# Attention with a maxout FFN on one core: K and Q through one transpose bank, two steps of software pipelining, weights in column halves

## The chip, the core and the metric

The kernel runs on one core of a Trainium2 chip. The metric is the device time of one execution in microseconds (us). Engines are named as in the profile's rows: PE is TensorE (PEld its weight loads), DVE is VectorE, ACT is ScalarE, POOL is GpSimd, SP is SyncE, which issues most transfers. [...]

## What is computed

```python
# q, k, v: (4, 8, 768, 64); n_sink = 4, window = 64; heads 0, 2 and 6 are "retrieval" heads
scores = q @ k.T / sqrt(64)
causal = rel >= 0                                    # rel = query position - key position
stream = causal & (key < n_sink | rel < window)
a = softmax(where(retrieval head, causal, stream), scores)
x = (a @ v).transpose(0, 2, 1, 3).reshape(3072, 512)
h = maximum(maximum(x @ w1, x @ w2), x @ w3)         # w1, w2, w3: 512 x 768
out = h @ w_out                                      # w_out: 768 x 512, out 3072 x 512
```

## The kernel before

The work is cut into 32 **steps**. Step s is a batch entry, a half of its 768 tokens (384, three blocks of 128) and a pair of heads; four steps (four pairs of heads) make a half, two halves a batch entry. A **first-half step** has 384 queries on 384 keys (two score units), a **second-half step** 384 queries on 768 keys (four score units). When a half's four steps are done, its 384 x 512 rows of x go through the FFN, which is cut into 24 **units** by a generator (`ffn`, L206): 18 times four matmuls of 384 columns, for three weight matrices and six blocks of 128 hidden columns, and three output tiles of six matmuls of 512 columns that count two units each. FFN units are laid between the pieces of later steps by `share` (L410), which spreads 168 units evenly over steps 7 to 32; the last half's 24 come behind everything.

The schedule is manual: every engine executes its instructions in the order in which the program writes them, so the loop at L424 sets the order on every queue. One pass s of that loop:

- `load(s + 7)` (L108): K, Q and V of a step, four transfers on SyncE's queue, into a pool of 8.
- `prep(s + 1)` (L269): VectorE casts K and Q to fp16 (`kn`, `qn`).
- `scores(s, [0, 1])` (L313): score matmuls on TensorE into PSUM tiles `st` (a pool of two), exponentials on ScalarE into `pt`, masks by GpSimd's multiplications with `mk`.
- `av(s - 1)` (L360): probabilities times V on TensorE into `oacc`; VectorE's reciprocal `rc` and product `x`.
- `scores(s, [2, 3])` in second-half steps.
- `turn_x(s - 1)` (L387): three transposes of x on TensorE into `tr`, a copy to `xT` by VectorE.
- `turn(s + 1, 1)` and `turn(s + 1, 0)` (L292): for K, then for Q, three transposes into `tr` and a copy to `KT` or `QT` by VectorE, whose result has a stride of three elements.
- `prep_v(s + 1)` (L278): V to fp16 by VectorE (`va`), and GpSimd's product `vf` of V with the far mask `fm`, for key blocks that are far from the query.

Between the pieces stand five calls of `share`. The pool `trp` holds one PSUM bank, so each of the three turns of a step waits until the copy of the one ahead has emptied it. The FFN's PSUM pool `fsp` holds two tiles; ScalarE takes away the first matrix's product (`acc`, L231) and the output tiles (`ot`, L248), VectorE takes the two maxima (L234). In steps 0 to 3 `head_consts` (L177) adds, per pair of heads, four mask operations of 256 columns and the copy `fm` on VectorE. The weights are four transfers that GpSimd issues, three behind step 0 and one behind step 2.

Of the kernel before, what the change touches and what calls it, by code (L numbers as in the profile page):

```python
# [48 lines left out]
def kernel(  # L49
# [14 lines left out]
    nc = tc.nc  # L64
# [24 lines left out]
    xp = ctx.enter_context(tc.tile_pool(name="xp", bufs=2))  # L89
# [37 lines left out]
    load(0)  # L127
    ir32 = consts.tile([P, 2 * H], mybir.dt.int32, name="ir32")
    nc.sync.dma_start(
# [3 lines left out]
    for s in range(1, AHEAD):  # L133
        load(s)


    ident = consts.tile([P, P], FP16, name="ident")
    make_identity(nc, ident)
# [8 lines left out]
    win = consts.tile([P, 256], FP16, name="win")  # L147
    nc.gpsimd.affine_select(
        out=win, in_=base, compare_op=ALU.is_gt, fill=0.0,
        base=window, pattern=[[-1, 256]], channel_multiplier=1,  # L150
    )
    win0 = consts.tile([P, 256], FP16, name="win0")
    nc.vector.tensor_copy(out=win0, in_=win)
    if n_sink > 0:
        nc.vector.tensor_copy(out=win0[0:n_sink, :], in_=base[0:n_sink, :])
    full = consts.tile([P, 256], FP16, name="full")
    nc.vector.tensor_tensor(out=full, in0=base, in1=win, op=ALU.subtract)
    full0 = consts.tile([P, 256], FP16, name="full0")
    nc.vector.tensor_tensor(out=full0, in0=base, in1=win0, op=ALU.subtract)
# [6 lines left out]
    RT = consts.tile([P, H], FP32, name="RT")  # L166
    nc.vector.tensor_copy(out=RT, in_=ir32[:, 0 : 2 * H : 2])

    far = consts.tile([P, H, 4], FP32, name="far")
    nc.vector.tensor_copy(out=far, in_=RT.unsqueeze(2).to_broadcast([P, H, 4]))  # L170
    if n_sink > 0:
        nc.vector.memset(far[0:n_sink, :, 0:1], 1.0)

    mk = consts.tile([P, H, 512], FP16, name="mk")
    fm = consts.tile([P, H, 4, D + 1], FP16, name="fm")

    def head_consts(hp):  # L177
# [87 lines left out]
    KTs = {}  # L265
    QTs = {}
    cast = {}

    def prep(s):  # L269
        b, half, hp = where(s)  # L270
        ks_, qs, vs = staged.pop(s)
# [4 lines left out]
        cast[s] = (qn, kn, vs)  # L276

    def prep_v(s):  # L278
        b, half, hp = where(s)
        vs = cast[s][2]  # L280
        j, k0 = b % 2, half * HB
        hs = slice(2 * hp, 2 * hp + 2)
        if s < NHP:
            head_consts(hp)
        nc.vector.tensor_copy(out=va[j][:, hs, k0 : k0 + HB, 0:D], in_=vs)  # L285
# [6 lines left out]
    def turn(s, which):  # L292
        b, half, hp = where(s)
        src = cast[s][which]
        tr = trp.tile([P, 1024], FP16, tag="tr", name="tr")
        for j in range(HB):
            nc.tensor.transpose(  # L297
                tr[:, j * P : (j + 1) * P], src[:, j].rearrange("p h d -> p (h d)"), ident
            )
        if which == 0:  # L300
            t = QTs[s] = qkt.tile([P, HALF], FP16, tag="QT", name="QT")
        else:
            if half == 0:
                KTs[b, hp] = qkt.tile([P, S], FP16, tag=f"KT{hp}", name=f"KT{hp}")
            t = KTs[b, hp][:, half * HALF : (half + 1) * HALF]
        nc.vector.tensor_copy(  # L306
            out=t.rearrange("p (t j) -> p j t", j=HB),
            in_=tr[:, 0:HALF].rearrange("p (j t) -> p j t", j=HB),
        )
# [3 lines left out]
    def scores(s, us):  # L313
        b, half, hp = where(s)
        QT, KT = QTs[s], KTs[b, hp]
# [4 lines left out]
        for u in us:  # L320
            st = sps.tile([P, 2, 512], FP32, tag="st", name="st")
            sts.append(st)
            for ki, q0, n, c0 in UNITS[half][u]:
                for hl in range(2):
                    hb = D * hl
                    nc.tensor.matmul(  # L326
                        st[:, hl, c0 : c0 + n * P],
                        KT[hb : hb + D, ki * P : (ki + 1) * P],
                        QT[hb : hb + D, q0 * P : (q0 + n) * P],
                        start=True, stop=True,  # L330
                    )
# [72 lines left out]

    FIRST = 7
    units = (2 * B - 1) * 24
    done = 0.0
    emitted = 0

    def share(s, part, parts):  # L410
        nonlocal emitted
        if s < FIRST or s >= NSTEP + 1:
            return
        want = units * ((s - FIRST) + (part + 1) / parts) / (NSTEP + 1 - FIRST)
        n = int(want) - emitted
        if n > 0 and queue:
            fill(n)
            emitted += n

    prep(0)  # L420
    turn(0, 1)
    turn(0, 0)
    prep_v(0)
    for s in range(NSTEP + 1):  # L424
# [66 lines left out]
```

## Time and profile before

| | |
|---|---|
| median of 3 runs | 281.4 us (280.76 to 281.68) |
| profiled execution: time | 280.9 us |
| profiled execution: span (first to last instruction) | 280.8 us |
| busy: PE, PEld, DVE, ACT, POOL | 214.8, 125.8, 179.3, 117.9, 126.5 us |
| chain that ended last, by engine | PE 58%, DVE 27%, issue 5%, ACT 4% |
| first scores of steps 0, 5, 8, 31 start at | 9.78, 45.66, 70.81, 249.14 us |
| HBM read, written | 25.17 MB, 6.29 MB |

The profile is one execution. A row of the timeline gives start, duration, engine, line, operation, output and inputs, and in brackets how long the engine was idle before and what ended that. Matmuls are pipelined and their ends modelled, so a matmul's cost in a row of them is read from start to start.

### The profile page before, as it was taken

The numbers are of one execution on the slowest core, as the hardware profiler recorded it, in microseconds if no ns is written. First come the engines' busy times: TensorE is split into PE (matmuls) and PEld (weight loads), VectorE is DVE, ScalarE is ACT, GpSimd is POOL, SyncE is SP. The second block draws the span as 40 slices with busy tenths as digits, with TensorE's granted clock in tenths as the row PEclk, the third lists the DMA queues.
The fourth block names the chain that finished last, engine by engine and source line by source line (L and its number), as shares of the span: only waits on it lengthen the run. The fifth ranks groups of instructions, "written<-read, shape, count | busy, mean of one in ns | idle before, by whom it ended". The sixth has DMA issues, their size and how long they took to land.

```text
span 280.8 us, 5222 instructions
## 1 busy us (share of the span) xinstructions
PE 214.8 (76%) x2000; PEld 125.8 (45%) x2000; DVE 179.3 (64%) x381; ACT 117.9 (42%) x169; POOL 126.5 (45%) x141
## 2 busy tenths in 40 slices
PE   0333366668888889889898888897788878989994
PEld 0222234435554545454445444554455435555551
DVE  2878855455786776667767774667668853664360
ACT  1222234553334364565244357653342347553322
POOL 2366455444555543455455454446354445253000
PEclk9999999999999999999999999999999999999999
DMA  6999999321103920293017511720020011000202
GB/s 159 268 280 213 220 247 259 96 66 51 30 0 105 275 73 4 87 251 98 16 58 220 151 25 75 215 78 2 37 76 2 0 40 75 4 0 2 112 0 112
DMA packets 49000, 28.65 MB, mean 102 GB/s; under 512 B 27216, under 2 KB 45904, under 8 KB 48976
## 3 DMA queue, kind: packets, MB, share of 16 engines
q1 hardware_dynamic: 46608, 25.18, 32.1%
q0 software_dynamic: 2368, 3.15, 6.3%
q8 instruction: 15, 0.25, 0.4%
q14 instruction: 9, 0.07, 0.1%
HBM read 25.17 MB, written 6.29 MB: 112 GB/s over the span
## 4 chain that ended last, share of the span: by engine, by line
PE 58%; DVE 27%; issue 5%; ACT 4%; DMA 2%; SPq 2%; POOL 0%; DVEq 0%; ACTq 0%
PE yy L223 21%; PE yy L241 10%; PE st L326 8%; PE oacc L371 7%; PE tr L297 7%; DVE QT L306 5%; DVE KT L306 5%; DVE xT L399 3%; DVE acc L234 3%; ACT pt L334 3%; DVE mk L180 3%; DVE hT L234 3%; PE yst L223 2%; PE tr L396 2%; DVE x L381 1%
## 5 line engine op out<-in xcount | busy, mean ns | idle before, releaser
L356 POOL TENSOR_TENSOR pt<-pt,mk 128x512 f16<-128x512 f16 (+1 forms) x96 | 100.7, 1071 | 56.9 <-ACT pt L334 56.7
L334 ACT ACTIVATE pt<-st 128x1024 f16<-128x1024 f32 x96 | 82.8, 917 | 75.6 <-PE st L326 71.0
L287 POOL TENSOR_TENSOR vf<-va,fm 128x390 f16<-128x390 f16 (+1 forms) x32 | 20.9, 654 | 71.7 <-DVE va L285 71.7
L231 ACT CAST acc<-yy 128x384 f16<-128x384 f32 x45 | 21.7, 482 | 51.2 <-PE yy L223 46.8
L326 PE MATMUL st<-QT,KT 64*128 64x384 f16 (+2 forms) x320 | 31.2, 309 | 13.7 <-DVE QT L306 13.3
L234 DVE TENSOR_TENSOR acc<-yy,acc 128x384 f16<-128x384 f32 x45 | 25.0, 556 | 22.2 <-PE yy L223 14.8
L223 PE MATMUL yy<-xT,w0t 128*128 128x384 f16 x180 | 37.4, 331 | 0.1
L223 PE MATMUL yy<-xT,w2t 128*128 128x384 f16 x180 | 36.6, 326 | 0.8 <-ACT acc L231 0.6
L223 PE MATMUL yy<-xT,w1t 128*128 128x384 f16 x180 | 37.2, 330 | 0.0
L306 DVE COPY KT<-tr 128x384 f16<-128x384 f16 x32 | 25.6, 801 | 13.7 <-PE tr L297 13.5
L297 PE MATMUL tr<-ident,kn 128*128 128x128 f16 x96 | 11.7, 238 | 27.9 <-DVE xT L399 19.1
L306 DVE COPY QT<-tr 128x384 f16<-128x384 f16 x32 | 25.5, 798 | 10.5 <-PE tr L297 10.5
L241 PE MATMUL yy<-woutt,hT 128*128 128x512 f16 x132 | 31.8, 379 | 0.0
L371 PEld LDWEIGHTS <-pt 128*128 128x128 f16 x672 | 27.6, 104 | 6.2 <-issue 2.3
L371 PE MATMUL oacc<-va,pt 128*128 128x65 f16 x352 | 28.3, 204 | 0.0
L326 PEld LDWEIGHTS <-KT 64*128 64x128 f16 x320 | 13.8, 100 | 32.0 <-issue 18.1
L234 DVE TENSOR_TENSOR hT<-yy,acc 128x384 f16<-128x384 f32 x45 | 24.9, 554 | 4.4 <-PE yy L223 2.8
L248 ACT COPY ot<-yy 128x512 f32<-128x512 f32 x22 | 12.9, 588 | 26.2 <-PE yy L241 23.4
L371 PE MATMUL oacc<-vf,pt 128*128 128x65 f16 x320 | 23.7, 203 | 0.0
L297 PEld LDWEIGHTS <-kn 128*128 128x128 f16 x96 | 8.6, 105 | 32.1 <-issue 23.0
L223 PEld LDWEIGHTS <-w2t 128*128 128x128 f16 x192 | 17.2, 97 | 11.7 <-issue 2.9
L223 PEld LDWEIGHTS <-w0t 128*128 128x128 f16 x192 | 16.9, 98 | 11.8 <-issue 3.4
(44 smaller groups left out, 185.1 us busy)
## 6 DMA issues: line engine op xcount, KB each, us to landing
ks<-in_k_dram SPq DMA_DIRECT2D x32, 192.0 KB, 3.8
qs<-in_q_dram SPq DMA_DIRECT2D x32, 192.0 KB, 4.0
vs<-in_v_dram SPq DMA_DIRECT2D x64, 96.0 KB, 3.8
out_dram<-ot SPq DMA_DIRECT2D x24, 256.0 KB, 2.0
w0t<-in_moe_w_dram POOLq DMA_DIRECT2D x1, 768.0 KB, 9.9
w1t<-in_moe_w_dram POOLq DMA_DIRECT2D x1, 768.0 KB, 13.9
w2t<-in_moe_w_dram POOLq DMA_DIRECT2D x1, 768.0 KB, 17.8
woutt<-in_moe_w_out_dram POOLq DMA_DIRECT2D x1, 768.0 KB, 10.7
```

What stands on the lines that cost most here:

```text
L223: nc.tensor.matmul(yy[:, 0:HALF], w_t[wi][:, ks, ni * P : (ni + 1) * P], xT[b, half][ks], start=(ks == 0), stop=(ks == KS - 1),)
L231: nc.scalar.copy(out=acc, in_=yy[:, 0:HALF])
L234: nc.vector.tensor_tensor(out=dst, in0=yy[:, 0:HALF], in1=acc, op=ALU.max)
L241: nc.tensor.matmul(yo[:, 0:DMdl], hT[ns][:, tb * P : (tb + 1) * P], woutt[:, ns, :], start=(ns == 0), stop=(ns == NNB - 1),)
L248: nc.scalar.copy(out=ot, in_=yo[:, 0:DMdl])
L287: nc.gpsimd.tensor_tensor(out=vf[j][:, hs, k0:k1, 0 : D + 1], in0=va[j][:, hs, k0:k1, 0 : D + 1], in1=fm[:, hs, k0:k1], op=ALU.mult,)
L297: nc.tensor.transpose(tr[:, j * P : (j + 1) * P], src[:, j].rearrange("p h d -> p (h d)"), ident)
L306: nc.vector.tensor_copy(out=t.rearrange("p (t j) -> p j t", j=HB), in_=tr[:, 0:HALF].rearrange("p (j t) -> p j t", j=HB),)
L326: nc.tensor.matmul(st[:, hl, c0 : c0 + n * P], KT[hb : hb + D, ki * P : (ki + 1) * P], QT[hb : hb + D, q0 * P : (q0 + n) * P], start=True, ...
L334: nc.scalar.activation(out=pt[:, u, :, 0:w], in_=st[:, :, 0:w], func=AF.Exp, scale=sc)
L356: nc.gpsimd.tensor_tensor(out=x, in0=x, in1=m, op=ALU.mult)
L371: nc.tensor.matmul(o[:, qi, hl, 0 : D + 1], pt[:, u, hl, c : c + P], vv[:, 2 * hp + hl, ki, 0 : D + 1], start=(idx == 0), stop=(idx == len ...
```

## The change

K and Q of a step are transposed into one bank one after the other and leave it by one copy of 768 columns, into one tile `KQ` (`turn(s)`). Casts run two steps ahead instead of one, and Q's cast is ScalarE's. The transposes of x belong to step s - 2 and stand right behind the first scores; K and Q of step s + 1 are turned before AV instead of at the end of the step. FFN units are spread from step 5 instead of 7, with weights of 5 for a first-half and 7 for a second-half step. Masks are one operation of 512 columns per head; `fm` goes, its place in the product `vf` is taken by `far`, broadcast. V's cast in the first four steps is ScalarE's. The weight matrices come in column halves, seven transfers behind step 1. The flags' transfer moves to ScalarE's queue.

```diff
-    xp = ctx.enter_context(tc.tile_pool(name="xp", bufs=2))
+    xp = ctx.enter_context(tc.tile_pool(name="xp", bufs=3))
...
-    load(0)
     ir32 = consts.tile([P, 2 * H], mybir.dt.int32, name="ir32")
-    nc.sync.dma_start(
+    nc.scalar.dma_start(
...
+    warm = consts.tile([P, 2], FP32, name="warm")
+    nc.vector.memset(warm, 0.0)
+    nc.scalar.activation(out=warm, in_=warm, func=AF.Exp)
...
+    def head_masks(hp):
+        for h in (2 * hp, 2 * hp + 1):
+            nc.vector.scalar_tensor_tensor(
+                out=mk[:, h], in0=F, scalar=RT[:, h : h + 1], in1=W,
+                op0=ALU.mult, op1=ALU.add,
+            )
...
-    def head_consts(hp):
...
+    def load_weights():
+        for c in (0, DF // 2):
+            for wt, w in zip(w_t, (moe_w1, moe_w2, moe_w3)):
+                nc.gpsimd.dma_start(
+                    out=wt[:, :, c : c + DF // 2],
+                    in_=w[:, c : c + DF // 2].rearrange("(ks p) n -> p ks n", p=P),
+                )
+        nc.gpsimd.dma_start(
+            out=woutt, in_=moe_w_out.rearrange("(ns p) m -> p ns m", p=P)
+        )
...
         nc.vector.tensor_copy(out=kn, in_=ks_.rearrange("p h j d -> p j h d"))
-        nc.vector.tensor_copy(out=qn, in_=qs.rearrange("p h j d -> p j h d"))
+        nc.scalar.copy(out=qn, in_=qs.rearrange("p h j d -> p j h d"))
...
+        if s < NHP:
+            nc.scalar.copy(out=vdst, in_=vs)
+        else:
+            nc.vector.tensor_copy(out=vdst, in_=vs)
...
-            in1=fm[:, hs, k0:k1], op=ALU.mult,
...
+            in1=far[:, hs, k0:k1].unsqueeze(3).to_broadcast([P, 2, k1 - k0, D + 1]),
+            op=ALU.mult,
...
+    def turn(s):
         tr = trp.tile([P, 1024], FP16, tag="tr", name="tr")
+        for i, x in enumerate(cast.pop(s)):
+            for j in range(HB):
+                c = i * HALF + j * P
+                nc.tensor.transpose(
+                    tr[:, c : c + P], x[:, j].rearrange("p h d -> p (h d)"), ident
+                )
+        half = where(s)[1]
+        KQs[s] = qkt.tile(
+            [P, S], FP16, tag=f"KQ{half}", name="KQ", bufs=2 if half else NHP + 3
+        )
         nc.vector.tensor_copy(
+            out=KQs[s].rearrange("p (i t j) -> p i t j", i=2, j=HB),
+            in_=tr[:, 0:S].rearrange("p (i j t) -> p i t j", i=2, j=HB),
         )
...
+    FIRST = NHP + 1
+    weight = [0 if s < FIRST else (5, 7)[where(s)[1]] for s in range(NSTEP)] + [3]
...
-        if s + 1 < NSTEP:
-            prep(s + 1)
         if live:
             n_u = len(UNITS[where(s)[1]])
             scores(s, [0, 1])
-        share(s, 0, 5)
-        if s > 0:
+        if s > 1:
+            turn_x(s - 2)
+        share(s, 1, 7)
+        if s + 1 < NSTEP:
+            turn(s + 1)
+        share(s, 3, 7)
+        if 0 < s <= NSTEP:
             av(s - 1)
-        share(s, 1, 5)
+        if s + 2 < NSTEP:
+            prep(s + 2)
         if live and n_u > 2:
             scores(s, [2, 3])
...
         if s + 1 < NSTEP:
+            prep_v(s + 1)
+        if s + 2 < NHP:
+            head_masks(s + 2)
+        share(s, 6, 7)
+        if s == 1:
+            load_weights()
```

VectorE's queue over one first-half step in the middle of the program, before. The rows run from the copy of x (`xT`) of one step to that of the next; the maxima of FFN units are the rows of L234:

```order
L399 COPY xT_1958<-tr 128x384
L306 COPY KT_1971<-tr 128x3x128
L306 COPY QT<-tr 128x3x128
L285 CAST va_164<-vs 128x2x3x64
L274 CAST kn<-ks 128x384
L275 CAST qn<-qs 128x384
L379 RECIPROCAL rc<-oacc 128x6
L381 TENSOR_TENSOR x<-oacc,rc 128x384
L234 TENSOR_TENSOR acc<-yy,acc 128x384
L399 COPY xT_1959<-tr 128x384
```

The same queue over a first-half step now (maxima are the rows of L230):

```order
L399 COPY xT_1998<-tr 128x384
L230 TENSOR_TENSOR acc<-yy,acc 128x384
L303 COPY KQ<-tr 128x768
L230 TENSOR_TENSOR hT_1909<-yy,acc 128x384
L379 RECIPROCAL rc<-oacc 128x6
L381 TENSOR_TENSOR x<-oacc,rc 128x384
L268 CAST kn<-ks 128x384
L281 CAST va_171<-vs 128x2x3x64
L230 TENSOR_TENSOR acc<-yy,acc 128x384
L230 TENSOR_TENSOR hT_1910<-yy,acc 128x384
L399 COPY xT_1999<-tr 128x384
```

The two copies of K and Q behind the copy of x became one, a maximum stands between, and `qn` is gone from this queue.

GpSimd's queue around the weights, before, from `vf` of step 1 to the first mask of step 1:

```order
L287 TENSOR_TENSOR vf0_166<-va0_164,fm_176 128x2x3x65
L194 DMA w0t_177<-in_moe_w1_dram 128x4x768
L194 DMA w1t_178<-in_moe_w2_dram 128x4x768
L194 DMA w2t_179<-in_moe_w3_dram 128x4x768
L356 TENSOR_TENSOR pt_262<-pt_262,mk_175 128x2x256
```

The same queue now, from `vf` of step 2 to its last transfer:

```order
L283 TENSOR_TENSOR vf0_173<-va0_171,far_167 128x2x3x65
L191 DMA w0t_177<-in_moe_w1_dram 128x4x384
L191 DMA w1t_178<-in_moe_w2_dram 128x4x384
L191 DMA w2t_179<-in_moe_w3_dram 128x4x384
...
L195 DMA woutt_180<-in_moe_w_out_dram 128x6x512
L356 TENSOR_TENSOR pt_311<-pt_311,mk_170 128x2x256
```

The three transfers moved behind `vf` of step 2 and became six of half the width (the second three read like the first), `woutt` follows at once, and the masks of step 2 stand behind all seven.

## Rows read from the trace of the kernel before

**Rows 1.** The page, part 1: busy time, share of the span, instructions.

```profile
PE 214.8 (76%) x2000; PEld 125.8 (45%) x2000; DVE 179.3 (64%) x381; ACT 117.9 (42%) x169; POOL 126.5 (45%) x141
```

**Rows 2.** Windows: busy us of PE, PEld, DVE, ACT, POOL; clock, DMA share, GB/s.

```profile
0.00:45.66 45.66, 16.27 (x135) 9.39 (x136) 30.89 (x71) 10.89 (x13) 23.76 (x33) 1.00 1.04 234
...
70.81:249.14 178.33, 151.50 (x1467) 88.79 (x1467) 123.40 (x260) 84.23 (x124) 87.61 (x93) 1.00 0.27 79
```

**Rows 3.** Waits of PE from 61 to 261 us: total us, times, longest us.

```profile
PE tr L297 <- DVE xT L399: 16.4, 24, 1.3
PE st L326 <- DVE QT L306: 6.2, 16, 0.9
PE tr L297 <- DVE KT L306: 4.6, 14, 0.9
```

**Rows 4.** Timeline of PE, a first-half step (19): start, us, what.

```profile
153.01 0.50 PE L326 MATMUL st<-QT,KT 64*128 64x384 f16 x6 [0.24 <-DVE QT L306]
153.45 0.82 PE L223 MATMUL yy<-xT,w2t 128*128 128x384 f16 x4
154.11 0.35 PE L371 MATMUL oacc<-va,pt 128*128 128x65 f16 x6
...
154.48 0.81 PE L223 MATMUL yy<-xT,w0t 128*128 128x384 f16 x4
...
157.58 0.33 PE L297 MATMUL tr<-ident,kn 128*128 128x128 f16 x3 [0.75 <-DVE xT L399]
157.75 0.81 PE L223 MATMUL yy<-xT,w0t 128*128 128x384 f16 x4
```

**Rows 5.** Timeline of PE, a second-half step (13).

```profile
107.65 0.61 PE L326 MATMUL st<-QT,KT 64*128 64x384 f16 x8 [0.24 <-DVE QT L306]
108.19 0.82 PE L223 MATMUL yy<-xT,w2t 128*128 128x384 f16 x4
...
109.50 0.23 PE L371 MATMUL oacc<-vf,pt 128*128 128x65 f16 x2
...
110.45 0.81 PE L223 MATMUL yy<-xT,w1t 128*128 128x384 f16 x4
```

**Rows 6.** Timeline of DVE in the middle of the program.

```profile
157.18 0.35 DVE L399 COPY xT<-tr 128x384 f16<-128x384 f16 x1
...
159.16 0.80 DVE L306 COPY QT<-tr 128x384 f16<-128x384 f16 x1 [0.42 <-PE tr L297]
159.82 0.34 DVE L285 CAST va<-vs 128x384 f16<-128x384 f32 x1
...
160.72 0.56 DVE L234 TENSOR_TENSOR hT<-yy,acc 128x384 f16<-128x384 f32 x1
161.19 0.54 DVE L274 CAST kn<-ks 128x384 f16<-128x384 f32 x1
...
162.13 0.20 DVE L379 RECIPROCAL rc<-oacc 128x6 f32<-128x6 f32 x1
```

**Rows 7.** Groups of ACT by line and form: count, busy us, mean ns, idle before.

```profile
L334 ACT ACTIVATE pt<-st 128x1024 f16<-128x1024 f32 x64 | 63.8, 1024 | 75.6 <-PE st L326 71.0 <-POOL vf L287 4.6
```

**Rows 8.** Timeline of POOL at the start.

```profile
17.81 0.90 POOL L287 TENSOR_TENSOR vf<-va,fm 128x390 f16<-128x390 f16 x1 [2.16 <-DVE va L285]
18.65 0.94 POOL L194 DMA_DIRECT2D w0t<-in_moe_w_dram  x1
...
20.32 0.75 POOL L194 DMA_DIRECT2D w2t<-in_moe_w_dram  x1
21.08 2.89 POOL L356 TENSOR_TENSOR pt<-pt,mk 128x512 f16<-128x512 f16 x3
```

**Rows 9.** The page, part 6: issues, KB each, us from issue to landing.

```profile
w2t<-in_moe_w_dram POOLq DMA_DIRECT2D x1, 768.0 KB, 17.8
```

**Rows 10.** Timeline of PE where the first FFN unit stands (step 7).

```profile
61.36 1.46 PE L223 MATMUL yy<-xT,w0t 128*128 128x384 f16 x4
...
65.54 0.55 PE L326 MATMUL st<-QT,KT 64*128 64x384 f16 x6
```

**Rows 11.** Timeline of PE, start of the last half's FFN.

```profile
261.09 0.81 PE L223 MATMUL yst<-xT,w0t 128*128 128x384 f16 x4
```

More of the change, by code (lines that the diff above doesn't have):

```diff
@@ L132 @@
     )
-    for s in range(1, AHEAD):
+    for s in range(AHEAD):
         load(s)
-    ident = consts.tile([P, P], FP16, name="ident")
-    make_identity(nc, ident)
+    warm = consts.tile([P, 2], FP32, name="warm")
+    nc.vector.memset(warm, 0.0)
+    nc.scalar.activation(out=warm, in_=warm, func=AF.Exp)
     base = consts.tile([P, 256], FP16, name="base")
@@ L146 @@
     )
-    win = consts.tile([P, 256], FP16, name="win")
+    W = consts.tile([P, 512], FP16, name="W")
     nc.gpsimd.affine_select(
-        out=win, in_=base, compare_op=ALU.is_gt, fill=0.0,
+        out=W[:, 0:256], in_=base, compare_op=ALU.is_gt, fill=0.0,
         base=window, pattern=[[-1, 256]], channel_multiplier=1,
     )
-    win0 = consts.tile([P, 256], FP16, name="win0")
-    nc.vector.tensor_copy(out=win0, in_=win)
+    ident = consts.tile([P, P], FP16, name="ident")
+    make_identity(nc, ident)
+    nc.vector.tensor_copy(out=W[:, 256:512], in_=W[:, 0:256])
     if n_sink > 0:
[L155 to L159, printed above, removed]
+        nc.vector.tensor_copy(out=W[0:n_sink, 256:512], in_=base[0:n_sink, :])
+    F = consts.tile([P, 512], FP16, name="F")
+    for c in (0, 256):
+        nc.vector.tensor_tensor(
+            out=F[:, c : c + 256], in0=base, in1=W[:, c : c + 256], op=ALU.subtract
+        )
+    RT = consts.tile([P, H], FP32, name="RT")
+    nc.vector.tensor_copy(out=RT, in_=ir32[:, 0 : 2 * H : 2])
+    far = consts.tile([P, H, 4], FP16, name="far")
+    nc.vector.tensor_copy(out=far, in_=RT.unsqueeze(2).to_broadcast([P, H, 4]))
+    if n_sink > 0:
+        nc.vector.memset(far[0:n_sink, :, 0:1], 1.0)
+    mk = consts.tile([P, H, 512], FP16, name="mk")
+    def head_masks(hp):
[4 more added lines that the diff above has]
+            )
     va = [consts.tile([P, H, NSB, VW], FP16, name=f"va{j}") for j in range(2)]
@@ L288, in prep_v @@
             out=vf[j][:, hs, k0:k1, 0 : D + 1], in0=va[j][:, hs, k0:k1, 0 : D + 1],
-            in1=fm[:, hs, k0:k1], op=ALU.mult,
-        )
-    def turn(s, which):
-        b, half, hp = where(s)
-        src = cast[s][which]
+            in1=far[:, hs, k0:k1].unsqueeze(3).to_broadcast([P, 2, k1 - k0, D + 1]),
+            op=ALU.mult,
+        )
+    def turn(s):
         tr = trp.tile([P, 1024], FP16, tag="tr", name="tr")
[L296 to L305, printed above, removed]
+        for i, x in enumerate(cast.pop(s)):
[7 more added lines that the diff above has]
+            [P, S], FP16, tag=f"KQ{half}", name="KQ", bufs=2 if half else NHP + 3
+        )
         nc.vector.tensor_copy(
-            out=t.rearrange("p (t j) -> p j t", j=HB),
-            in_=tr[:, 0:HALF].rearrange("p (j t) -> p j t", j=HB),
+            out=KQs[s].rearrange("p (i t j) -> p i t j", i=2, j=HB),
+            in_=tr[:, 0:S].rearrange("p (i j t) -> p i t j", i=2, j=HB),
         )
@@ L314, in scores @@
         b, half, hp = where(s)
-        QT, KT = QTs[s], KTs[b, hp]
+        KQ = KQs[s]
+        KT = [KQs[s - half * NHP], KQ]
         if 0 in us:
@@ L327, in scores @@
                         st[:, hl, c0 : c0 + n * P],
-                        KT[hb : hb + D, ki * P : (ki + 1) * P],
-                        QT[hb : hb + D, q0 * P : (q0 + n) * P],
+                        KT[ki // HB if half else 0][
+                            hb : hb + D, ki % HB * P : (ki % HB + 1) * P
+                        ],
+                        KQ[hb : hb + D, HALF + q0 * P : HALF + (q0 + n) * P],
                         start=True, stop=True,
@@ L411, in share @@
         nonlocal emitted
-        if s < FIRST or s >= NSTEP + 1:
+        if s > NSTEP:
             return
-        want = units * ((s - FIRST) + (part + 1) / parts) / (NSTEP + 1 - FIRST)
-        n = int(want) - emitted
-        if n > 0 and queue:
+        want = units * (sum(weight[:s]) + weight[s] * (part + 1) / parts) / sum(weight)
+        n = int(want + 1e-6) - emitted
+        if n > 0:
             fill(n)
             emitted += n
+    head_masks(0)
     prep(0)
-    turn(0, 1)
-    turn(0, 0)
+    turn(0)
+    head_masks(1)
+    prep(1)
     prep_v(0)
-    for s in range(NSTEP + 1):
+    for s in range(NSTEP + 2):
         live = s < NSTEP
```

56 lines of the change are left out of this document (5 added, 51 removed).

## The prediction

> **What bounds the kernel now.** The page's first part comes first: TensorE is busy 76% of the span and VectorE 64%, nothing else comes near [rows 1]. A busy share hides stages, so the windows view is read next, cut at the first score matmuls of steps 5, 8 and 31 [rows 2]. Before step 5 (45.66 us) TensorE is busy 16.27 us and VectorE 30.89: that stretch is a chain through VectorE and GpSimd with no FFN work in it. From step 8 to step 31 (178.33 us, 23 steps) TensorE is the pacing engine, but not a full one. The waits of TensorE over the middle name what it waits for: VectorE's copies out of the transpose bank, xT 16.4 us, QT 6.2 us, KT 4.6 us, 27.2 us in all [rows 3].
>
> The timeline of TensorE gives what a step costs without waits, from start to start. One FFN unit (four 384-column matmuls, or half an output tile) is 154.11 - 153.45, about 0.65 us. A first-half step has scores 0.44 us, the AV product 154.48 - 154.11 = 0.37 us, and three groups of three transposes at 157.75 - 157.58 = 0.17 us: 1.31 us [rows 4]. A second-half step has scores 0.54 us and AV 0.95 us [rows 5]; its second scores have 1,792 columns against 1,536, estimated at 0.51 us; with transposes 2.5 us. Steps 8 to 30 carry 155 units: 155 x 0.65 + 12 x 1.31 + 11 x 2.5 = 144 us of work in 178.3. So **about 34 us, 1.5 us per step, is TensorE standing still**, most of it in the three copies: the one transpose bank is filled and emptied three times per step, in a row.
>
> **The change, part by part.** *One bank, one copy, two steps ahead.* The K and Q transposes follow each other without a wait, and one copy of 768 columns replaces two of 384. Its result is wanted only at the next step's scores, after AV and at least two units. The x transposes belong to a step two back, so x is long ready, and one or two units lie between them and the bank's next use, 0.65 to 1.3 us against the 0.75 us that a wait for xT took [rows 4]. All three waits of rows 3 lose their cause. What is late next is VectorE's own queue, which TensorE meets through the two PSUM tiles of the FFN: unit n cannot start before the result of unit n-2 is taken away.
>
> So the price of the large copy matters. No row shows it. A 384-column copy is 0.80 us busy, and the next starts 0.66 us after it [rows 6]. Twice that, **1.32 us**, is taken, since it is the same stride and source. The bounds are 0.70 us (twice the contiguous xT copy, 0.35 us) and 1.60 us. [...]
>
> *A first-half step.* From the end of the K and Q transposes VectorE has, in the order shown above: the copy 1.32, one unit's max 0.47, reciprocal 0.20, x (taken like a max) 0.47, kn 0.45, va 0.25 us, 3.2 us, and only then the next unit's max [rows 6]; kn and va count 0.09 us less than their busy time, as the max does (0.56 busy, the next 0.47 later). TensorE has meanwhile one unit, AV and three units. The last unit needs the tile that this late max frees: it could start 0.65 + 0.37 + 1.3 = 2.3 us behind the transposes and starts at 0.1 + 3.2 + 0.47 = 3.8, 1.5 us late. Where that earlier unit is one that ScalarE empties (one in three, and output tiles) it is 0 to 0.3 us. Mean 0.9 us.
>
> *A second-half step.* Two places. ScalarE does two exponentials of about 1 us right after the scores [rows 7], and an acc cast behind them comes 0.7 to 1.2 us late; later the seventh unit waits for the fifth's max, which is queued behind reciprocal, x, kn and va, or for the fifth's cast behind the second pair of exponentials. Walking the three phases of the unit cycle through these queues gives about 1.6, 1.4 and 0.6 us, less with output tiles: 1.0 us.
>
> *qn to ScalarE.* 32 casts of some 0.5 us leave VectorE. ScalarE had 84.23 us in the 23 middle steps [rows 2], 3.7 a step, and gets 4.2: it stays covered by TensorE's 6.2 us of work. VectorE in a first-half step has the 3.2 us, xT 0.3 and 1.5 more maxes, 4.2 us in all, of TensorE's 4.56: it fits with little air, and that is why stalls remain.
>
> *Loads.* The flags' transfer leaves SyncE's queue, so later loads are issued 0.5 us earlier; casts run one step further ahead of loads that are issued seven ahead. Priced at nothing: the loads of the middle steps are hidden by these seven steps.
>
> *GpSimd.* Same masks; the vf product reads a stride-0 operand in place of fm. It is 0.90 us now [rows 8] and taken at that; below, nothing is gained from one operand fewer to fetch; above, twice, 0.9 us per first-half step, still inside 4.56 us.
>
> *Start.* Step 0's scores move from 9.78 us to about 8.7: the casts run side by side and one copy is gone, against two masks placed ahead of kn. The 512-wide mask op saves VectorE little and the fm copies go. Then GpSimd paces: masks of step 0 from 9.7 us, 2.9 us a step, and vf 0.9 us, so it is done with vf of step 2 at 17.7 (a wait of 0.4 us for the exponentials of step 1 included). There stand now seven weight transfers instead of three; three took 21.08 - 18.65 = 2.43 us [rows 8], so seven at the 0.75 us of the later ones, and 0.2 more for the first, cost 5.4 us, to 23.1. Masks 2, vf 3 and masks 3 end at 29.8 us. AV of step 3 waits for them and the second scores of step 4 stand behind it, 2 x (0.37 + 0.51) = 1.7 us at the lower clock. **Step 5 starts at 31.5 us instead of 45.66.** Bounds 28 (an issue of half the bytes at half the price) to 36 us (vf at twice, late loads).
>
> *Weights.* w2t landed 17.8 us after its issue at 20.32, so three matrices took 19.5 us from 18.65 [rows 9]. Three halves are half of it: about 10 us from 17.7, ahead of the first FFN unit at 32; the others, and woutt, are wanted 10 and 20 units later. Not on the path.
>
> *FFN from step 5 instead of 7*, 7 units in a second-half step, 5 in a first-half one, 3 at the end. Steps 5 to 31: 15 x (2.5 + 4.55) + 12 x (1.31 + 3.25) = 160.5 us. The first units run at the lower TensorE clock, as now: the four matmuls at 61.36 were 1.46 us busy [rows 10] against 0.82 later; with the AV between them and the wait for step 3's xT, 3 us. Behind step 31 stand 3 units, AV and two x transposes, 3.3 us, and a wait for the last xT, 0.7: 4.0 us. The last half's FFN, from 261.09 to the end, does not change: 280.8 - 261.1 = 19.7 us [rows 11].
>
> **Sum.** 31.5 + 160.5 + (12 x 0.9 + 15 x 1.0 = 25.8) + 3 + 4.0 + 19.7 = 244.5 us, say **244 us** of span. The profiled execution had a span of 280.8 and a time of 280.9, the median of the runs is 281.4, half a microsecond more; it is left out.
>
> **Rivals.** *The stalls go almost wholly.* If the copy costs nearer its lower bound, 0.3 us per step remain: 244 - 27 x 0.65 = 227 us. For it: VectorE's load per step falls below TensorE's in both kinds of step. Against: first-half steps leave 0.3 us.
>
> *VectorE's queue becomes the bound, or the start stays long.* With the copy at 1.6 us and casts slowed by GpSimd, stalls of 1.5 us per step, what they are now: 244 + 27 x 0.55 = 259; with step 5 at 36 us, 263. For it: two PSUM tiles and an in-order queue; VectorE is busy 123.40 of 178.33 us in the middle steps already, 69% [rows 2]. Against: VectorE's work per step falls by about one cast.
>
> [...]
>
> That the change does not do what it says is excluded by the order: VectorE has 299 instructions for 383.
>
> **Numbers.** Forecast (stalls of 0.6 to 1.3 us per step, step 5 at 29 to 34 us): 0.62, by itself 233 to 254 us. Stalls gone: 0.16, 224 to 233. VectorE or a long start: 0.19, 254 to 268. Lower clock: 0.02. A loss elsewhere that eats all: 0.01. The range that leaves out half of either neighbour's outer part is 229 to 261 us. About 0.3%, 0.8 us, is what can be told from no change: faster 0.97, same 0.01, slower 0.02.
>
> **What would show it.** Waits of TensorE on xT, KT and QT near nothing; the 768-column copy at 1.3 to 1.5 us busy; step 5's scores at 29 to 34 us; first-half steps of 5.3 to 5.7 us and second-half ones of 7.7 to 8.3 us; FFN matmuls waiting for VectorE's max or ScalarE's acc, which they hardly do now. Wrong it would be if step 5 came after 38 us, if the copy took 2 us, or if FFN matmuls ran at the lower clock for more than some 10 us.

## The result, and the profile after

**244.64 us**, the median of 4 runs (243.73 to 244.81), against 281.08 us before on the same chip: ratio 0.870 (0.867 to 0.873), 36.4 us less. The forecast was 244.0 us. By stages, first scores to first scores, the sum of the prediction stands against the trace so:

| stage | forecast | measured |
|---|---|---|
| start, to step 5 | 31.5 | 33.51 |
| step 5 (7.05 + 1.0 + 3) | 11.05 | 10.54 |
| steps 6 to 30 (13 x 8.05 + 12 x 5.46) | 170.2 | 166.57 |
| step 31 to the end (8.05 + 4.0 + 19.7) | 31.75 | 32.48 |
| span | 244.5 | 243.1 |

The terms miss by +2.0, -0.5, -3.6 and +0.7 us and cancel down to -1.4. In every run the time lies 1.7 to 1.8 us above the span, here 244.76 against 243.1. The table before has 0.1, since its two figures are not of one execution: the run of 280.90 us had a span of 279.2 us, and the trace spans 280.8. So the forecast left out 1.7 us where it spoke of half a microsecond; with them it is 246.2 us, and part of the agreement of the medians is luck.

Part 1 of the page [rows 1 before]:

```profile
PE 206.3 (85%) x2000; PEld 122.2 (50%) x2000; DVE 147.4 (61%) x302; ACT 132.0 (54%) x206; POOL 128.5 (53%) x144
```

The windows, cut at those first scores (columns as in [rows 2]):

```profile
0.00:33.51 33.51, 14.21 (x131) 9.18 (x132) 22.72 (x44) 15.20 (x25) 24.87 (x34) 1.00 1.07 234
33.51:44.05 10.54, 10.27 (x81) 5.76 (x80) 4.74 (x11) 5.68 (x8) 5.12 (x6) 1.00 1.24 208
44.05:210.62 166.57, 154.28 (x1574) 91.47 (x1573) 107.84 (x225) 100.19 (x156) 94.24 (x101) 1.00 0.36 102
210.62:243.10 32.48, 27.56 (x216) 15.78 (x215) 12.07 (x24) 10.90 (x18) 4.26 (x5) 1.00 0.13 49
```

TensorE's busy time fell by 8.5 us only; VectorE's fell by 32 (casts of Q gone, cheaper copies), ScalarE's rose by 14. What went is TensorE's standing still. Its waits from 30 to 225 us [rows 3 before]:

```profile
PE yy L219 <- ACT acc L227: 5.9, 12, 0.7
PE yy L219 <- DVE acc L230: 3.6, 4, 1.1
PE tr L296 <- DVE xT L399: 2.3, 4, 0.9
```

The 27 us on xT, QT and KT are down to 2.3 us on xT; the waits that are left belong to the FFN's two PSUM tiles, on ScalarE's cast and VectorE's max.

Two costs that the prediction had to estimate. The copy out of the transpose bank, from the groups of DVE by line (count, busy us, mean ns, idle before):

```profile
L303 DVE COPY KQ<-tr 128x768 f16<-128x768 f16 x32 | 30.5, 954 | 14.0 <-PE tr L296 14.0
```

and Q's cast, from the groups of ACT:

```profile
L269 ACT CAST qn<-qs 128x384 f16<-128x384 f32 x32 | 16.6, 518 | 4.2 <-DMA qs<-in_q_dram 4.2
```

The copy of 768 columns takes 0.95 us, not 1.32; qn takes 0.52 us, as estimated.

The start, on POOL's timeline [rows 8 before]:

```profile
10.15 2.88 POOL L356 TENSOR_TENSOR pt<-pt,mk 128x512 f16<-128x512 f16 x3 [0.46 <-ACT pt L334]
13.00 0.83 POOL L283 TENSOR_TENSOR vf<-va,far 128x390 f16<-128x390 f16 x1
14.38 3.40 POOL L356 TENSOR_TENSOR pt<-pt,mk 128x512 f16<-128x512 f16 x3 [0.55 <-ACT pt L334]
17.75 1.28 POOL L283 TENSOR_TENSOR vf<-va,far 128x390 f16<-128x390 f16 x1
18.97 0.94 POOL L191 DMA_DIRECT2D w0t<-in_moe_w_dram  x1
...
23.57 0.88 POOL L195 DMA_DIRECT2D woutt<-in_moe_w_out_dram  x1
24.41 2.94 POOL L356 TENSOR_TENSOR pt<-pt,mk 128x512 f16<-128x512 f16 x3
27.25 0.88 POOL L283 TENSOR_TENSOR vf<-va,far 128x390 f16<-128x390 f16 x1
```

on DVE's, up to the turn of step 3:

```profile
4.47 0.88 DVE L175 SCALAR_TENSOR_TENSOR mk<-F,RT,W 128x512 f16<-128x512 f16 x1
...
8.26 1.98 DVE L175 SCALAR_TENSOR_TENSOR mk<-F,RT,W 128x512 f16<-128x512 f16 x2
...
16.98 2.59 DVE L175 SCALAR_TENSOR_TENSOR mk<-F,RT,W 128x512 f16<-128x512 f16 x2
19.49 0.34 DVE L399 COPY xT<-tr 128x384 f16<-128x384 f16 x1
20.73 0.96 DVE L303 COPY KQ<-tr 128x768 f16<-128x768 f16 x1 [0.89 <-PE tr L296]
```

Seven weight issues hold GpSimd from 18.97 to 24.41 us, 5.4 us as forecast; the masks of step 2 end at 27.3 us. TensorE's timeline has a wait for xT of step 0, which stands behind the masks on VectorE, one for GpSimd's masks of step 2, and one of step 5's first scores, for exponentials of step 4:

```profile
19.89 0.48 PE L296 MATMUL tr<-ident,kn 128*128 128x128 f16 x3 [2.67 <-DVE xT L399]
...
27.40 0.35 PE L371 MATMUL oacc<-va,pt 128*128 128x65 f16 x3 [1.37 <-POOL pt L356]
...
33.51 1.31 PE L324 MATMUL st<-KQ 64*128 64x384 f16 x8 [0.80 <-ACT pt L334]
```

### The profile page after: what moved, and what is told of

Read it like the earlier page. It is cut to its first block, busy times and chain, and to the rows that moved or that the text cites. A ratio compares the mean times of both kernels' runs of the same rounds, so it can differ in the third digit from the quotient of the medians.

```text
span 243.1 us, 5176 instructions
## 1 busy us (share of the span) xinstructions
PE 206.3 (85%) x2000; PEld 122.2 (50%) x2000; DVE 147.4 (61%) x302; ACT 132.0 (54%) x206; POOL 128.5 (53%) x144
## 4 chain that ended last, share of the span: by engine, by line
PE 48%; DVE 16%; ACT 9%; POOL 9%; issue 8%; DMA 6%; SPq 3%; POOLq 0%; DVEq 0%; ACTq 0%
PE yy L219 19%; PE yy L237 9%; POOL pt L356 7%; PE oacc L371 7%; ACT pt L334 6%; PE st L324 4%; DVE kn L268 4%; DMA ks<-in_k_dram 3%; PE tr L296 3%; DVE acc L230 3%; PE yst L219 2%; DMA qs<-in_q_dram 2%; DVE va L281 2%; DVE mk L175 2%; ACT acc L227 2%
## 5 line engine op out<-in xcount | busy, mean ns | idle before, releaser
L230 DVE TENSOR_TENSOR acc<-yy,acc 128x384 f16<-128x384 f32 x45 | 25.0, 555 | 26.9 <-PE yy L219 13.5
L303 DVE COPY KQ<-tr 128x768 f16<-128x768 f16 x32 | 30.5, 954 | 14.0 <-PE tr L296 14.0
L324 PE MATMUL st<-KQ 64*128 64x384 f16 (+2 forms) x320 | 29.9, 297 | 4.9 <-DVE KQ L303 3.6
L371 PEld LDWEIGHTS <-pt 128*128 128x128 f16 x672 | 26.3, 100 | 7.2 <-POOL pt L356 3.5
L371 PE MATMUL oacc<-va,pt 128*128 128x65 f16 x352 | 26.7, 199 | 2.9 <-POOL pt L356 2.8
L230 DVE TENSOR_TENSOR hT<-yy,acc 128x384 f16<-128x384 f32 x45 | 25.0, 555 | 5.8 <-PE yy L219 3.5
L283 POOL TENSOR_TENSOR vf<-va,far 128x390 f16<-128x390 f16 (+1 forms) x32 | 20.7, 648 | 11.9 <-DVE va L281 6.0
L219 PEld LDWEIGHTS <-w1t 128*128 128x128 f16 x192 | 17.9, 98 | 15.6 <-issue 6.4
L219 PEld LDWEIGHTS <-w0t 128*128 128x128 f16 x192 | 17.8, 99 | 14.9 <-issue 5.7
L399 DVE COPY xT<-tr 128x384 f16<-128x384 f16 x32 | 11.4, 356 | 19.9 <-PE tr L396 19.6
L296 PE MATMUL tr<-ident,kn 128*128 128x128 f16 x96 | 11.7, 237 | 13.4 <-DVE kn L268 8.1
L324 PEld LDWEIGHTS <-KQ 64*128 64x128 f16 x320 | 11.9, 98 | 20.3 <-issue 11.2
L371 PE MATMUL oacc<-vf,pt 128*128 128x65 f16 x320 | 21.7, 194 | 0.0
```

Source lines behind the costliest of these rows:

```text
L219: nc.tensor.matmul(yy[:, 0:HALF], w_t[wi][:, ks, ni * P : (ni + 1) * P], xT[b, half][ks], start=(ks == 0), stop=(ks == KS - 1),)
L230: nc.vector.tensor_tensor(out=dst, in0=yy[:, 0:HALF], in1=acc, op=ALU.max)
L283: nc.gpsimd.tensor_tensor(out=vf[j][:, hs, k0:k1, 0 : D + 1], in0=va[j][:, hs, k0:k1, 0 : D + 1], in1=far[:, hs, k0:k1].unsqueeze(3).to_br ...
L296: nc.tensor.transpose(tr[:, c : c + P], x[:, j].rearrange("p h d -> p (h d)"), ident)
L303: nc.vector.tensor_copy(out=KQs[s].rearrange("p (i t j) -> p i t j", i=2, j=HB), in_=tr[:, 0:S].rearrange("p (i j t) -> p i t j", i=2, j=HB),)
L324: nc.tensor.matmul(st[:, hl, c0 : c0 + n * P], KT[ki // HB if half else 0][hb : hb + D, ki % HB * P : (ki % HB + 1) * P], KQ[hb : hb + D, ...
```

## The experiments

The theory after the result: the gain has three parts, the copies' cost (and how they walk through memory), the K and Q turns and the x turn taken off TensorE's path, and an earlier start of FFN work; the 20 us of stalls that are left are VectorE's and ScalarE's queues, met through the FFN's two tiles. The rivals: one part alone makes the gain; the copy's length sets the stalls that are left; the start sets them.

**e1_before_dense: the kernel before, with only the walk of the copies changed.** The diff holds an edit that the prediction had passed over: the result was written with a stride of three elements and the bank read in order; now the result is written in order, and the bank is read in groups of three elements that lie 128 elements apart.

```diff
-            out=t.rearrange("p (t j) -> p j t", j=HB),
-            in_=tr[:, 0:HALF].rearrange("p (j t) -> p j t", j=HB),
+            out=t.rearrange("p (t j) -> p t j", j=HB),
+            in_=tr[:, 0:HALF].rearrange("p (j t) -> p t j", j=HB),
```

> The kernel before, its K and Q copies walking through the result in order (dense writes, strided reads of the bank) instead of writing with a stride of three. Theory: the order of the walk, not the number of columns, set the 0.80 us of a 384-column copy, since the changed kernel moves 768 columns in 0.95 us. Then the copies fall to about 0.55 us; the five start-up steps lose 2 x 0.25 us each, 2.5 us, and TensorE's waits on KT and QT in the middle (10.8 us) lose about 6: some 273 us, ratio 0.97. Rival: a PSUM copy of 384 columns has that price whatever its walk: 0.80 us and 281 us.

271.99 us (270.15 to 272.42), ratio 0.964 (0.959 to 0.969). The copies:

```profile
L306 DVE COPY KT<-tr 128x384 f16<-128x384 f16 x32 | 17.8, 558 | 13.6 <-PE tr L297 13.3
```

0.56 us in place of 0.80 [rows 6], 64 of them with Q's, and the kernel before gains 10 us by this edit alone.

**e8_before_merged: the kernel before, with one bank and one copy** for K and Q (in order, as changed), at the old place and one step ahead.

```diff
...
-        for j in range(HB):
-            nc.tensor.transpose(
-                tr[:, j * P : (j + 1) * P], src[:, j].rearrange("p h d -> p (h d)"), ident
...
+        for i, x in enumerate((kn, qn)):
+            for j in range(HB):
+                c = i * HALF + j * P
+                nc.tensor.transpose(
+                    tr[:, c : c + P], x[:, j].rearrange("p h d -> p (h d)"), ident
...
```

> The kernel before with K and Q through one bank and one copy of 768 columns, at the place where K was turned; nothing else (one step of pipelining, casts on VectorE, FFN from step 7). Theory that the bank's three turns in a row were the main loss: waits on KT and QT go (10.8 us in the middle and what follows them, 1.2 us in each start-up step), 262 us, ratio 0.93; TensorE still waits about 16 us on xT. Rival, that the waits only move to xT and to the scores behind the longer copy: 272 us or more.

264.34 us (263.26 to 265.73), ratio 0.937 (0.931 to 0.943): 7.7 us under e1. KT and QT are gone from the waits; xT stays whole at 16.5 us, 24 times (61 to 255 us).

```profile
PE tr L302 <- DVE xT L405: 16.5, 24, 1.3
```

**e5_one_step: the changed kernel, with x turned one step back** again, behind the second scores, and K and Q behind it, so that both moves are taken back together.

```diff
-        if s > 1:
-            turn_x(s - 2)
         share(s, 1, 7)
-        if s + 1 < NSTEP:
-            turn(s + 1)
-        share(s, 3, 7)
...
+        share(s, 3, 7)
+        if 0 < s <= NSTEP:
+            turn_x(s - 1)
         if s + 1 < NSTEP:
+            turn(s + 1)
             prep_v(s + 1)
```

> The changed kernel with the turns of x one step back and at the end of the step, as before: FFN units, AV, second scores, FFN units, then x of step s - 1 and K and Q of step s + 1 through the bank. One bank, casts two steps ahead, FFN from step 5 and everything else stay. Theory that the second step of pipelining has its own share: TensorE waits again for xT, 0.75 us and its refill in each of 27 steps, and for KQ at the scores: 262 us, ratio 0.93. Rival, that the merged bank and the earlier FFN start were all of it: 247 us or less.

265.49 us (264.89 to 266.27), ratio 0.944 (0.939 to 0.949), 20.9 us above the change. The wait for xT is back (50 to 245 us):

```profile
PE tr L296 <- DVE xT L399: 18.5, 25, 1.3
```

So the order of the turns is the largest of the parts that were taken out one at a time. Everything else in the change together, without it, brings 15 us, and the merged copy alone (e8) some 18: with the old order nothing else in the change shows a gain beyond the copy. That holds for the start too. Step 5 begins at 45.66 us before, 41.90 in e8, 37.07 in e5 and 33.51 in the changed kernel; e5 is 4.8 us ahead of e8 there and yet no faster in the end. Which of the masks and casts makes those 4.8 us was not tried.

**e2_after_strided: the changed kernel with the old walk** of its copy (in order read, stride of three written).

```diff
-            out=KQs[s].rearrange("p (i t j) -> p i t j", i=2, j=HB),
-            in_=tr[:, 0:S].rearrange("p (i j t) -> p i t j", i=2, j=HB),
+            out=KQs[s].rearrange("p (i t j) -> p i j t", i=2, j=HB),
+            in_=tr[:, 0:S].rearrange("p (i j t) -> p i j t", i=2, j=HB),
```

> The changed kernel, its 768-column copy writing with a stride of three as the kernel before did. Expected price of the copy 1.4 to 1.6 us instead of 0.95. Theory A, as predicted: TensorE's remaining stalls come through VectorE's queue and the two FFN tiles, so 0.55 us more per step shows in about half: 27 x 0.3 = 8 us, some 252 us, ratio 0.897. Rival B: the remaining stalls come from ScalarE's casts and the copy is covered: 244.6 us within 1.5.

248.6 us (247.73 to 249.0), ratio 0.882 (0.878 to 0.886).

```profile
L303 DVE COPY KQ<-tr 128x768 f16<-128x768 f16 x32 | 46.4, 1451 | 14.0 <-PE tr L296 14.0
```

A copy 0.5 us longer costs 4 us in all, not 27 x 0.5. From step 16 on the steps of a round last 5.18, 5.95, 5.99, 5.29, 7.77, 7.87, 8.01, 8.72 us, against 5.18, 5.51, 5.96, 4.87, 7.36, 7.87, 8.01, 8.71 in the changed kernel: three steps in eight show it, and only one of the second-half ones. The same edit was worth 10 us in the kernel before (e1).

**e4_qn_vector: the changed kernel with Q's cast on VectorE again.**

```diff
-        nc.scalar.copy(out=qn, in_=qs.rearrange("p h j d -> p j h d"))
+        nc.vector.tensor_copy(out=qn, in_=qs.rearrange("p h j d -> p j h d"))
```

> The changed kernel with Q's cast back on VectorE. Theory A, VectorE's queue is what TensorE meets: half of 0.46 us in each of 27 steps and 0.5 us in each start-up step, 252 us, ratio 0.895. Rival B: since the large copy takes 0.95 us and not 1.32 there is room, and ScalarE's acc casts gain what VectorE loses: 244.6 us within 1.5.

253.35 us (252.38 to 253.88), ratio 0.900 (0.896 to 0.904), 8.7 us above the change. The wait of FFN matmuls for VectorE's max grows (45 to 230 us):

```profile
PE yy L219 <- DVE hT L230: 5.8, 4, 1.5
PE yy L219 <- ACT acc L227: 4.9, 9, 0.7
```

Again not in every step: steps 21 and 23 grow from 7.87 and 8.71 to 8.97 and 10.00 us, step 22 stays at 8.01.

**e7_whole_weights: the changed kernel with four whole weight transfers** instead of seven.

```diff
-        for c in (0, DF // 2):
-            for wt, w in zip(w_t, (moe_w1, moe_w2, moe_w3)):
...
+        for wt, w in zip(w_t, (moe_w1, moe_w2, moe_w3)):
+            nc.gpsimd.dma_start(out=wt, in_=w.rearrange("(ks p) n -> p ks n", p=P))
```

> The changed kernel with the weights in four whole transfers instead of seven, at the same place. GpSimd's issues take 3.3 instead of 5.6 us, so masks 2 and all behind them come 2.3 us earlier and step 5 starts near 31 us. The third matrix lands some 18 us after its issue, about 38.5 us, and the unit that wants it is due near 36: theory that the halves pay: 245 to 248 us. Rival, that the issue time costs more than the halves bring: 242.5 us, ratio 0.862.

245.11 us (243.26 to 246.43), ratio 0.870 (0.864 to 0.877): no difference from the change. Step 5 starts at 31.47 us, 2.0 earlier, as three issues less on GpSimd should make it, and lasts 14.29 us instead of 10.54, with a wait for the third matrix, behind which TensorE's matmuls take longer for a while: a unit 1.17 us at 39.82 and six score matmuls 0.93 us at 42.57, against 0.81 and 0.55 us in the changed kernel (39.49 and 41.17 us):

```profile
39.16 0.82 PE L215 MATMUL yy<-xT,w2t 128*128 128x384 f16 x4 [2.53 <-DMA w2t<-in_moe_w_dram]
39.82 1.17 PE L215 MATMUL yy<-xT,w0t 128*128 128x384 f16 x4
```

The halves buy the early units and pay for them with their issues.

**e3_casts_last: the changed kernel with kn, qn and va behind the last units of a step**, from step 5 on, so that rc and x have no casts between them and the next max. GpSimd's `vf` moves with them.

```diff
-        if s + 2 < NSTEP:
+        if s < FIRST and s + 2 < NSTEP:
             prep(s + 2)
...
         share(s, 6, 7)
+        if s >= FIRST and s + 2 < NSTEP:
+            prep(s + 2)
+        if s >= FIRST and s + 1 < NSTEP:
+            prep_v(s + 1)
```

> The changed kernel; from step 5 on the casts of K, Q and V of the coming steps stand behind the step's last FFN units instead of ahead of them. Theory A: the maxima of the last units no longer queue behind kn and va (0.7 us) on VectorE nor acc behind qn on ScalarE; stalls fall from some 0.8 to 0.4 us per step: 234 us, ratio 0.83. Rival B: the stalls are those of acc behind the exponentials and of only two FFN tiles, or the late vf holds up AV: 244 us or more.

241.93 us (241.14 to 242.72), ratio 0.859 (0.855 to 0.862): between the two expectations, 2.7 us gained of some 10. First-half steps lose up to 0.55 us (5.96 to 5.41), second-half steps next to nothing.

**e6_ffn_from7: FFN units from step 7 on, evenly**, as the kernel before spread them.

```diff
-    FIRST = NHP + 1
-    weight = [0 if s < FIRST else (5, 7)[where(s)[1]] for s in range(NSTEP)] + [3]
+    FIRST = NHP + 3
+    weight = [0 if s < FIRST else 1 for s in range(NSTEP)] + [1]
```

> The changed kernel with FFN units from step 7 on, spread evenly, as before. Total TensorE work is the same, so only what TensorE cannot fill in steps 5 and 6 is lost: two steps of about 5 us with 2.5 us of work each, and the low clock two steps longer: 244.6 + 6 = 251 us, ratio 0.89. Rival: steps 5 and 6 shrink to their work and nothing is lost, 245 us.

242.39 us (241.5 to 242.77), ratio 0.861 (0.857 to 0.864). Both expectations missed: it is 2.2 us faster than the change. So either the even shares or the later start is better, and the next two take them apart.

**e6b_even: from step 5, but even** (six units a step); **e6c_from7_5to7: from step 7, but with the weights 5 and 7.** Each is one of the two lines above.

> The changed kernel with FFN units from step 5 as there, but six in every step and six at the end, instead of 5 in a first-half and 7 in a second-half step. Theory C (the stalls come from the shares 5 and 7, which add up to 24 in four steps, so each round meets the queues of VectorE and ScalarE in the same bad places, the second-half steps above all): second-half steps fall to 7.0 us or less, first-half ones rise to about 6.0, and the time is 236 to 241 us, under the kernel that spreads from step 7 (242.4). Rival (what helped there was that steps 5 and 6 are free of FFN work): no better than the changed kernel, 244 to 247 us.

> The changed kernel with FFN units from step 7 and the weights 5 and 7 kept (7 to 32 then hold 168 units over a sum of 163, so shares of 5.15 and 7.2, which no longer add up to 24 in four steps). Theory C in the form that the evenness counts: second-half steps of about 8.2 us, 246 us or more. Theory C in the form that only the fixed phase of 24 units in four steps counts: near the even kernel, 242 to 243 us. Rival (the free steps 5 and 6 count): 242 us too, so this run tells only together with the even kernel from step 5.

e6b: 243.73 us (243.48 to 244.33), ratio 0.866 (0.862 to 0.870), hardly better than the change. e6c: **239.33 us** (238.23 to 239.72), ratio 0.849 (0.845 to 0.853), better than the even one. The text's sum is wrong: steps 7 to 32 weigh 154, not 163, so e6c's shares are 5.45 and 7.64. TensorE's waits from step 8 to step 31, first of e6b (59 to 209 us):

```profile
PE yy L219 <- ACT acc L227: 7.4, 16, 0.6
```

and of e6c (54.6 to 206.8 us):

```profile
PE yy L219 <- ACT acc L227: 2.5, 4, 0.7
PE yy L219 <- DVE acc L230: 1.3, 4, 0.8
PE yy L219 <- DVE hT L230: 0.9, 4, 0.3
```

In e6b every wait that the view lists is of one kind. Its timeline of TensorE in step 13 shows it twice, with w2t both times:

```profile
89.81 0.81 PE L219 MATMUL yy<-xT,w1t 128*128 128x384 f16 x4
90.89 0.81 PE L219 MATMUL yy<-xT,w2t 128*128 128x384 f16 x4 [0.27 <-ACT acc L227]
...
93.71 0.81 PE L219 MATMUL yy<-xT,w1t 128*128 128x384 f16 x4
95.15 0.81 PE L219 MATMUL yy<-xT,w2t 128*128 128x384 f16 x4 [0.62 <-ACT acc L227]
```

With six units a step the cycle of three matrices, through two tiles, meets the exponentials at the same point in every round; with 5 and 7 too, since four steps of each are 48 units, two whole FFNs (not 24 in four steps, as the expectations say). The steps of both kernels repeat every eight: those of the changed kernel stand with e2 above, e6b's last 5.86, 5.67, 5.57, 5.57, 5.99, 8.22, 7.86, 7.86 us; e6c's don't repeat. Standing time from step 8 to step 31, by the prediction's units (0.65 us each, and 43.2 us for scores, AV and transposes of 12 first-half and 11 second-half steps):

| kernel | units | work | time | standing |
|---|---|---|---|---|
| changed (5 and 7, from 5) | 137 | 132.3 | 151.1 | 18.9 |
| e6b (6, from 5) | 138 | 132.9 | 149.9 | 17.0 |
| e3 (5 and 7, from 5, late casts) | 137 | 132.3 | 149.0 | 16.7 |
| e6 (6.46, from 7) | 148.6 | 139.8 | 154.8 | 15.0 |
| e6c (5.45 and 7.64, from 7) | 149.5 | 140.4 | 152.1 | 11.8 |

Standing time is more than the waits in the rows (17.0 against 7.4 us in e6b): a wait counts there only from the modelled end of the matmul ahead, and a unit that is busy 0.81 us lets the next start after 0.65; the work is an estimate besides.

The free steps 5 and 6 don't make the gain themselves: e6c reaches step 8 only 4.8 us earlier (54.68 against 59.49 us) with 13.4 units, 8.7 us of work, less done, so 3.9 us are lost there. They come back, and more, because the same steps 8 to 31 stand 7 us less while they take 12 units more. At step 31 e6c is 3.8 us ahead, and its last stretch is 1.7 us shorter. What differs in steps 8 to 31 is the share alone; that it is the fixed phase, and not only the number of units in a step, is supported by e6b against e6 and by the repeating waits, but shares that wander from step 5 on were not tried.

**e10_even_casts: e6 and e3 together. e9_combined: these and e7's whole weights.**

> The changed kernel with even shares from step 7 (2.2 us faster alone) and the casts of K, Q and V behind the last units of a step from step 7 on (2.7 us faster alone). If the two take away different stalls (the even shares those of second-half steps, the late casts those of first-half ones): 239 to 240 us. If they take away the same: 241.5 to 242.5 us.

> As the last one, and the weights as three whole transfers and woutt instead of seven, behind step 1. With FFN work from step 7 instead of 5 the later arrival of w2 (about 4 us behind the halves) has no one waiting for it, and the 2 us that step 5 starts earlier with fewer issues on GpSimd should stay: 237 to 238.5 us. If the start is given back at the first units, as with the whole weights and FFN from step 5: 239 to 241 us.

e10: 242.25 us (239.28 to 242.31), ratio 0.858 (0.853 to 0.863), no better than e6 by its median. It stands less from step 8 on (12.9 us), but its step 7 lasts 9.37 us where e6's lasts 7.91, and single FFN matmuls there take up to 0.53 us, where none of e6's takes more than 0.34 (both from 43 to 60 us). e9: **238.27 us** (237.03 to 239.05), ratio 0.846 (0.842 to 0.850), faster than both kernels by 43 and 6 us. Here the issues saved stay saved: step 5 starts at 31.52 us, and no matmul waits for w2t. But of the 3.9 us by which its profiled execution is shorter than e10's only 2.2 are this start; step 7 lasts 7.91 us again, with no matmul of its units above 0.34 us, and whether the weights bring that about is not shown. e9 and e6c, which is the changed kernel with one number changed, can't be told apart.

## Why the prediction was right, and which of its terms were not

**The bound, right.** TensorE was read as the pacing engine that stands still in three copies in a row, and those waits did go. e5 and e8 show it from both sides: without the new order of the turns xT's 18.5 us come back, and with the merged copy alone 16.5 us stay. The size was read too small: steps 8 to 30 hold 6.46 units each, 149 and not 155 (the trace of the kernel before has 452 matmuls of L223 and 108 of L241 there), so TensorE stood still some 38 us, 1.7 a step, and not 34. The sum doesn't use this figure.

**The copy, mis-sized: 0.95 us for 1.32.** The wrong step is "Twice that, 1.32 us, is taken, since it is the same stride and source". The stride changed sides with the diff, and e1 and e2 show what that is worth: 0.56 for 0.80 us with 384 columns, 0.95 for 1.45 with 768. The forecast lost little by it, since the steps depend on the copy less than it thought: 0.5 us more makes 4 us in e2, three steps in eight. At that rate the 0.37 us too much are worth some 3 of the 3.6 us by which steps 6 to 30 came out below the forecast (an estimate).

**Stalls: right in sum, not in place.** Steps 6 to 30 hold 13 x 7.05 + 12 x 4.56 = 146.4 us of work and last 166.57: 20.2 us of standing, 0.81 us a step, for 23.8. In steps 16 to 23 it is 0.82 us in a first-half step and 0.94 in a second-half one, for 0.9 and 1.0. The waits are on the two queues that were named. But the mechanism gave each kind of step a mean, and the trace has a pattern that repeats to 0.01 us every eight steps; e2 and e4 lengthen single steps of it and leave their neighbours alone. For second-half steps two causes were given, a max queued behind reciprocal, x, kn and va, and an acc cast queued behind exponentials; e3, which takes kn and va out of the max's way, hardly moves those steps, and ScalarE's cast is the longer row of the waits. So the second cause looks the larger there; no run took it out alone.

**Start, 2.0 us late.** GpSimd paces it, as said: its rows follow each other without a gap from 14.38 to 32.55 us, its seven issues cost what was said, AV of step 3 and the second scores of step 4 take 1.73 us (30.99 to 32.72) for the 1.7 that was put as twice their cost in the middle, and three issues less bring step 5 forward by 2.0 us (e7). Two terms were too small. The issues begin at 18.97 us and not at 17.7: the masks of step 0 wait for exponentials until 10.15 us instead of 9.7, and GpSimd's own operations take longer beside VectorE's masks, 3.40 us for the masks of step 1 where those of step 0 take 2.88, and 1.28 us for `vf` of step 2 where step 1's takes 0.83. And at the end step 5's first scores wait 0.80 us for exponentials of step 4, which the sum did not hold. VectorE pays as well, also where GpSimd doesn't: two masks of 512 columns take 1.98 to 2.59 us in place of 0.88 + 0.73 = 1.6 alone. The turn of step 3 waits 2.67 us for the bank behind them, which looks worse, but GpSimd never stands still for it. "The 512-wide mask op saves VectorE little" was right, and no price was put on what it does to the engine beside it. This is read from the rows; no run moved the masks.

**FFN from step 5, taken as a gain, is none as made.** The sum gave steps 5 and 6 some 9 us of units to fill their gaps, and they do fill 3.9 us of gaps. It put no price on what the shares do to the rest of the program: e6c, with units two steps later, is 5.3 us faster. The likely reason is that 5 and 7 fix the phase of units and steps; it is not shown apart from the number of units in a step.

**Weights in halves, not on the path, right,** but only in exchange: e7 shows 2.0 us of start against 3.8 us of step 5, of which 2.53 are the wait; the rest goes with the longer matmuls behind it (six score matmuls 0.93 us for 0.55).

**The rivals.** VectorE's queue did not become the bound, but the margin is one cast: e4 puts Q's back and, with 253.35 us, comes just short of that rival's 254 to 268. TensorE's lower clock, given 0.02, did not last: four matmuls of a unit take 1.48 us at 35.05 and 0.81 at 39.49, some 4 us into FFN work, and the 3 us given for it in step 5 held.

## What to carry to other kernels

When an engine waits for a copy in every step, move what it copies a step further ahead as well as making the copy cheaper: taking the move out costs 21 us here, the cheaper walk alone brought 10 in the kernel before and 4 in the changed one, and without the move the rest of the change brought nothing beyond the merged copy. Read both sides of an access pattern in a diff; the same copy costs half as much again when it is the write that has the stride (0.80 us for 0.56, and 1.45 for 0.95). Where filler work is dealt to steps from a cycle (three matrices, two PSUM tiles), look for steps that repeat to the hundredth of a microsecond and try shares that don't divide the round: in e6c one number gained 5 us, though why is in part still a guess.

## What the hardware showed that was not expected

VectorE's copy from PSUM to SBUF of 384 columns of fp16 takes 0.35 us when it reads and writes in order (xT), 0.56 when it writes in order and reads three elements 128 apart, and 0.80 when it reads in order and writes with a stride of three; the last two are 0.95 and 1.45 us for 768 columns.

The clock column doesn't always tell TensorE's rate. In the changed kernel it reads 1.00 from the start on, and four matmuls take 1.48 us at 35.05 and 0.81 at 39.49. In e6c the column moves (windows of PE: busy us, clock, DMA share, GB/s), and once it has moved the matmuls follow it:

```profile
38.00:42.00 4.00, 2.29 (x28) 0.99 1.21 226
42.00:46.00 4.00, 3.20 (x42) 0.50 1.20 233
46.00:50.00 4.00, 3.91 (x27) 0.66 1.00 247
```

```profile
40.46 0.40 PE L324 MATMUL st<-KQ 64*128 64x384 f16 x4 [0.30 <-ACT pt L334]
...
45.43 1.31 PE L324 MATMUL st<-KQ 64*128 64x384 f16 x8 [0.80 <-ACT pt L334]
```

Four score matmuls are busy 0.40 us at 40.46, like the 0.39 of the four at 51.80, and eight 1.31 us at 45.43, where eight take 0.61 us in the changed kernel at 44.05. So TensorE was at its higher rate before FFN work began, fell again behind a window in which it was busy 2.29 of 4.00 us, and rose once more during the first units: the first, at 46.98 us, takes 1.49 us, just like the one at 35.05 above, and the third, at 49.47, 0.81.

VectorE's mask operation, with two tensors read from SBUF, took 0.73 to 0.88 us at 4.47 and 5.28 us, with GpSimd idle, and 1.0 to 1.3 us on the mean of a pair when GpSimd multiplied beside it; single ones took up to 1.43 us. GpSimd's mask products beside them took up to 1.67 us, for 1.15 in the median.

GpSimd's product vf takes 0.89 us on the mean with an operand of stride 0, and took 0.90 with a full one [rows 8]: the broadcast is free there.
